# A last chunk of 64 columns: two label steps side by side in the partitions, row tanh by transposes, two stores on another queue

## The chip, the cores and the metric

The kernel runs on one core of a Trainium2 chip. The time is the device time of one execution in microseconds; the kernel before has a median of 795.49 us over three runs (794.16 to 795.92). A profile of one more execution goes with it.

## The reference

A speech "joint" network, forward and backward, in bf16. x is (2, 16000, 256), g is (2, 8, 256), the incoming gradient is (2, 4000, 8, 256).

```
h  = gelu(conv3(x,  w1))[:, ::2, :]        # 16000 -> 8000 steps
f  = gelu(conv3(h,  w2))[:, ::2, :]        # 8000 -> 4000 steps
fe = f @ w_f ;  ge = g @ w_g               # (2,4000,256), (2,8,256)
j  = tanh(fe[:, :, None, :] + ge[:, None, :, :])   # (2,4000,8,256)
out = j @ w_o                              # (2,4000,8,256)
```

Returned are out and the gradients of x, w1, w2, g, w_f, w_g and w_o for the given gradient of out. The joint j has 8 label steps u for each of the 2 x 4000 time steps; its products with w_o, in both directions, and the gradient of w_o are most of the work.

## The kernel before, in words

**Tiling.** The 8000 time steps (both batches in a row) are cut into chunks: one of 256, fifteen of 512, and a last one of 64 (`sizes`). A chunk of 512 is held as A = 4 blocks of Pw = 128 steps, the last as A = 1 block of Pw = 64. Most tensors of a chunk stand with the features in the partitions and the steps in the free dimension (JT, FE, NGFE, GF, GHe, GHo and so on). Products that sum over time steps need the steps in the partitions; those copies are called rows and end in R (JR, FER, NFR, GFR, GHoR, GHeR, HRo, HRe, FR).

**Stages.** For each k the program records three stages, `stage_j(k)` (the joint), `stage_a(k+1)` (both convolutions, FE) and `stage_de(k-1)` (the backward pass through the convolutions and the weight gradients), so that in steady state three chunks are in work at once. At the end, `gg_out` makes the gradients of g, w_g and w_o.

**The joint of a chunk**, for each pair `up` of label steps u = 2 up and 2 up + 1: ScalarE makes JT = tanh(FE + GE) with the features in the partitions (L644). The same values with the steps in the partitions, JR, are made anew: VectorE adds FER and GEB (L668), ScalarE takes the tanh (L673). Chunks 0 and 1 (`TRANS`) instead transpose JT on TensorE into PSUM (L663) and copy the result out. TensorE then does, per pair: GWO += JR' x GO (the gradient of w_o, kept in one PSUM bank for the whole kernel), ps = WOT x GOT (the gradient with respect to j), out = JT' x WO. GO is the incoming gradient with the steps in the partitions, GOT its transpose by DMA. VectorE multiplies by 1 - j^2 (JSQ, L716) into ZS and NGZ and adds up to NGFE (L730, L733); ScalarE or VectorE copies out of PSUM to OUT_SB (L345, L350), and a DMA stores it.

In the last chunk one GO tile of 64 partitions holds all eight u (64 x 2048), one DMA transpose makes GOT from it, and each u is handled on its own with 64 partitions: out is 64 x 512 per pair (two u in the free dimension), GWO takes four matmuls per pair with 64 rows of JR each.

**stage_de** goes NGFE -> (WFT) GF -> (W2T) GHe, GHo -> (W1T) the gradient of x (GX_SB, stored by `put`), with the row copies NFR, GFR, GHeR, GHoR made on the way for the weight gradients: NFR with FR, GFR with HRe and HRo, GHoR and GHeR with X (loaded by `load_x`). For all but the last chunk these rows are made by DMA transposes on SyncE's queue; they share two buffers (`rows`), so GHeR waits until NFR has been read and GHoR until GFR has. For the last chunk TensorE transposes them (L489). The sums of the weight gradients live in ACCF, ACC2 and ACC1 in SBUF (L772); with the last chunk VectorE writes them to `stage` tiles (L764), which are stored, all on SyncE's queue but the very last, which ScalarE issues.

**What sets the order.** Operations are recorded with a cost estimate and a due time; the planner `Flow.issue` plays the engines forward, picks at each step the operation that can start first (ties by due time), and so writes a fixed order for each engine. Each engine and each DMA queue then works strictly in that order. PSUM has seven banks handed out in any order; other tiles have one to three buffers per class. A few operations may run on either ScalarE or VectorE (`evac`, JSQ); the planner picks. So an edit in one stage can move instructions of its neighbours. Nearly all DMAs, loads, stores and transposes, go through SyncE's one queue (L360, L362). In the last 40 us that queue holds, in order: the last GO load, OUT stores, NFR, GOT, GFR, the X load of the second last chunk, GHeR, OUT stores, GHoR, HRo, GX stores, the X load of the last chunk (two DMAs, one of a single row), the two small stores of g's gradient (`JR` 8 x 256, of `gg_out`), and the stores of g_sq, stage and GX_SB.

Of the kernel before, what the change touches and what calls it, by code (L numbers as in the profile page):

```python
# [220 lines left out]
def kernel(  # L221
# [198 lines left out]
    def load_go(k, up, at, after=()):  # L420
        c = chunks[k]
        A, Pw = c.A, c.Pw
        GO = buf("go", [P, NB, 2, V], BF16, "GO")
        if c.last:

            dma("SP", lambda: GO[:Pw].rearrange("p a u v -> p (a u v)"),
                lambda: bass.AP(tensor=go_.tensor, offset=go_.offset + c.c0 * U * V, ap=[[U * V, Pw], [1, U * V]]),
                r=[], w=[GO], bytes_=Pw * U * V * 2, new=[GO], at=at, after=after)
            st[k]["GO"] = {up: GO for up in range(UP)}
            return  # L430
        dma("SP", lambda: GO[:Pw, 0:A].rearrange("p a u v -> p a (u v)"),
            lambda: bass.AP(tensor=go_.tensor, offset=go_.offset + (c.c0 * U + 2 * up) * V,
                            ap=[[A * U * V, Pw], [U * V, A], [1, 2 * V]]),
            r=[], w=[GO], bytes_=Pw * A * 1024, new=[GO], at=at, after=after, sub="go")
        st[k].setdefault("GO", {})[up] = GO

    def load_got(k, up, at):
# [4 lines left out]
        if c.last:  # L442
            dma("SP", lambda: GOT[:, :, :, :, :Pw].rearrange("p a u k c -> p (a u k) c"),
                lambda: GO[:Pw].rearrange("p a u v -> p (a u v)"), r=[GO], w=[GOT],
                bytes_=Pw * U * V * 2, new=[GOT], transpose=True, at=at)
# [92 lines left out]
    def stage_a(k, t0, dt):  # L538
# [45 lines left out]
        for mt in range(KT):  # L584
# [6 lines left out]
            evac(lambda mt=mt: FE[:, 0:A, mt, :Pw], lambda ps=ps: fl(ps[:, :W], A), W, r=[ps], w=[(FE, mt)])  # L591
        if k not in TRANS:
            S["FER"] = rows(k, "fer", "FER", FE, 0, A, [(FE, 0), (FE, 1)], pe=Pw, lag=0.0 if c.first else 500.0)
# [4 lines left out]

    n_gwo = sum(len(c.blk) for c in chunks) * U * KT
    gwo_cnt = [0]  # L600
# [27 lines left out]
    def stage_j(k, t0, dt, GEB):  # L628
# [3 lines left out]
        FE = S["FE"]  # L632

        def pair(up):
            F.now = tu = t0 + dt * up / UP
            q = dt / UP
            JT = buf("jt", [P, 2, KT, CW], BF16, "JT")
            GOT, GO = S["GOT"].pop(up), S["GO"].pop(up)
            u0 = up if c.last else 0
            for j in range(2):  # L640
                for mt in range(KT):
                    def jt(e, j=j, mt=mt):
                        for b, lo, hi, _ in c.segs:
                            nc.scalar.activation(  # L644
                                out=fl(JT[:, j, mt, :W], A)[:, :, lo:hi], in_=FE[:, 0:A, mt, lo:hi], func=ACT.Tanh,
                                bias=GE[:, b, mt, 2 * up + j:2 * up + j + 1], scale=1.0)
# [4 lines left out]
            for h, tbs in enumerate(halves):  # L651
                JR = buf("jr", [P, 2, 2, D], BF16, "JR")
                th = tu + q * (h / 2 - 0.5)
                n, lo, m = len(tbs), tbs[0][0], Pw
                if k in TRANS:
                    tr = psum(BF16)
# [27 lines left out]
                op("PE", c_pe([V] * (4 * n)), gwo, r=[JR, GO], w=[], at=tu + q * (h / 2 + 0.3), sub="gwo")  # L684
            OUT = buf("out", [P, NB, 2, V], BF16, "OUT_SB")
            for step in range(4):
# [5 lines left out]
                def gj(e, j=j, d2=d2, ps=ps):  # L692
                    for kt in range(KT):
                        mm(fl(ps[:, :W], A), WOT[:, kt, d2 * P:(d2 + 1) * P], GOT[:, u0:u0 + A, j, kt, :Pw], kt == 0, kt == KT - 1)
                if u and d2 == 0:
                    NGZ = buf("ngz", [P, KT, CW], FP32, "NGZ")
                op("PE", c_pe([W] * KT), gj, r=[GOT, WOT], w=[ps], new=[ps, NGZ] if u and d2 == 0 else [ps])
                if d2 == 0:
                    JSQ = buf("jsq", [P, KT, CW], BF16, "JSQ")

                    def jsq(e, j=j, JSQ=JSQ):
                        if e == "ACT":
                            nc.scalar.activation(out=JSQ[:, :, :W], in_=JT[:, j, :, :W], func=ACT.Square)  # L703
                        else:
                            nc.vector.tensor_tensor(out=JSQ[:, :, :W], in0=JT[:, j, :, :W], in1=JT[:, j, :, :W], op=ALU.mult)
                    op(("ACT", "DVE"), (c_act(KT * W), c_dve(KT * W, 0.5)), jsq, r=[(JT, (j, 0)), (JT, (j, 1))], w=[JSQ],
# [69 lines left out]
    def stage_de(k, t0, dt):  # L776
# [136 lines left out]
        for bl, m in c.sblk:  # L913
# [21 lines left out]
            if bl % 2 == 1 or bl == A - 1:  # L935
# [201 lines left out]
```

## Time and profile before

| | |
|---|---|
| median of the runs | 795.49 us (794.16 to 795.92) |
| the profiled execution | 793.3 us |
| its span, first to last instruction | 791.0 us |
| TensorE, VectorE, ScalarE busy | 773.1, 716.1, 727.0 us |
| SyncE's hardware DMA queue | 177.03 of 178.82 MB |
| granted TensorE clock | 0.998 |
| last chunk's first joint work on TensorE beside the chunk before | from 753.88 us |
| last idle stretch of TensorE ahead of its end | 1.09 us at 777.4 us, waiting for NGFE |
| VectorE's last instruction ends | 786.66 us |
| SyncE's last DMA issue | 787.80 us |

A line of the timeline reads: start in us, duration in us, engine, source line, operation, output<-inputs, shape, count. For TensorE the shape in front (128*64) is that of the stationary weights, partitions times columns, and the next that of the moving operand. Matmuls overlap, so their price is read from one start to the next and not from the durations. L336 is the helper that issues all matmuls but the transposes, L360 and L362 the helper that issues DMAs (SPq is SyncE's queue, ACTq ScalarE's). Brackets show idle time of the engine just before and what ended it.

### The profile page before, as it was taken

Reading aid. Unit: us, or ns where it says so; the run is one execution under the profiler, and the core shown is the slowest. Engines: PE = TensorE matmul, PEld = TensorE weight load, DVE = VectorE, ACT = ScalarE, POOL = GpSimd, SP = SyncE. Lnnn points to the kernel's source line nnn. Section 1 sums busy time; section 2 is a strip of 40 time slices with the busy share of each in tenths; the row PEclk is TensorE's granted clock in tenths of the full one; section 3 lists DMA queues with packets and bytes.
Section 4 is the critical chain, followed back from the end, with each engine's and each line's share of the span. In section 5 each row is a group of like instructions: output and inputs, shape, how many; then the busy total and the mean of one; then the engine's idle time right before and its main releaser. Section 6 shows DMA issues by size and latency. Waiting matters only on the chain.

```text
span 791.0 us, 15682 instructions
## 1 busy us (share of the span) xinstructions
PE 773.1 (98%) x5687; PEld 537.9 (68%) x5722; DVE 716.1 (91%) x1514; ACT 727.0 (92%) x1176; POOL 83.8 (11%) x227
## 2 busy tenths in 40 slices
PE   8989999999999999999999999999999999999996
PEld 6657577576675767767677675776767767577764
DVE  5899999897998989999999898989989899899874
ACT  6999999999999998999999998999999999898752
POOL 2110010201002011110101102010020110102010
PEclk9999999999999999999999999999999999999999
DMA  9999999999999899999999999998999999999874
GB/s 208 205 190 202 214 263 229 244 228 281 202 231 256 231 238 195 229 267 219 233 218 254 228 217 233 214 264 209 230 235 214 239 237 228 237 264 255 201 177 123
DMA packets 381809, 178.82 MB, mean 226 GB/s; under 512 B 307586, under 2 KB 375460, under 8 KB 379812
## 3 DMA queue, kind: packets, MB, share of 16 engines
q1 hardware_dynamic: 380516, 177.03, 99.8%
q8 instruction: 45, 0.74, 0.4%
q10 hardware_dynamic: 1056, 0.52, 0.2%
q14 instruction: 32, 0.26, 0.1%
q0 software_dynamic: 160, 0.27, 0.1%
HBM read 51.42 MB, written 50.34 MB: 129 GB/s over the span
## 4 chain that ended last, share of the span: by engine, by line
PE 72%; ACT 11%; DVE 9%; DMA 3%; issue 3%; SPq 1%; POOL 0%; DVEq 0%; ACTq 0%
PE ps L336 60%; PE GWO L336 10%; ACT JT L644 2%; DVE g_s L516 2%; ACT JSQ L703 2%; DMA GOT<-GO 2%; ACT g_sq L510 2%; PE psb L489 2%; DVE NGZ L716 1%; ACT OUT_SB L345 1%; ACT JR L673 1%; DVE g_sq L529 1%; SPq L360 1%; ACT HTo L513 1%; DMA XC<-in_x_dram 1%
## 5 line engine op out<-in xcount | busy, mean ns | idle before, releaser
L644 ACT ACTIVATE JT<-FE,GE 128x512 bf16<-128x512 bf16 (+4 forms) x288 | 180.7, 680 | 0.0
L716 DVE SCALAR_TENSOR_TENSOR NGZ<-JSQ,ps 128x512 f32<-128x512 bf16 (+3 forms) x252 | 149.7, 607 | 2.5 <-PE ps L336 2.0
L336 PE MATMUL ps<-WO,JT 128*128 128x256 bf16 (+1 forms) x1008 | 148.2, 273 | 1.3 <-DVE NGZ L716 1.3
L336 PE MATMUL ps<-GOT,WOT 128*128 128x512 bf16 (+2 forms) x544 | 146.5, 362 | 1.8 <-DMA GOT<-GO 1.6
L345 ACT CAST OUT_SB<-ps 128x512 bf16<-128x512 f32 (+1 forms) x210 | 123.0, 600 | 17.4 <-PE ps L336 17.3
L703 ACT ACTIVATE JSQ<-JT 128x1024 bf16<-128x1024 bf16 (+2 forms) x128 | 128.6, 1005 | 9.2 <-DVE NGZ L716 8.2
L336 PEld LDWEIGHTS <-JT 128*128 128x128 bf16 (+1 forms) x1008 | 98.2, 98 | 54.9 <-issue 2.0
L336 PE MATMUL GWO<-GO,JR 128*128 128x256 bf16 (+1 forms) x1008 | 130.8, 273 | 0.1
L673 ACT ACTIVATE JR<-JR 128x1024 bf16<-128x1024 bf16 (+1 forms) x116 | 121.6, 1054 | 4.1 <-DVE JR L668 3.8
L733 DVE TENSOR_TENSOR ZS<-ZS,NGZ 128x1024 f32<-128x1024 f32 (+2 forms) x102 | 115.1, 1128 | 0.3
L336 PEld LDWEIGHTS <-JR 128*128 128x128 bf16 (+1 forms) x1008 | 98.2, 98 | 17.8 <-issue 1.3
L516 DVE SCALAR_TENSOR_TENSOR g_s<-g_sq,ps 128x512 bf16<-128x512 bf16 (+2 forms) x102 | 65.2, 639 | 41.0 <-ACT HTo L513 32.2
L336 PEld LDWEIGHTS <-W 128*128 128x128 bf16 x612 | 58.1, 98 | 59.5 <-issue 2.2
L336 PE MATMUL ps<-XC,W 128*128 128x512 bf16 (+2 forms) x408 | 84.3, 362 | 0.9 <-DMA XC<-in_x_dram 0.9
L668 DVE TENSOR_TENSOR JR<-FER,GEB 128x1024 bf16<-128x1024 bf16 (+1 forms) x116 | 79.2, 684 | 2.2 <-PE GWO L336 1.0
L336 PEld LDWEIGHTS <-X 128*128 128x128 bf16 (+1 forms) x756 | 73.8, 98 | 9.4
L772 DVE TENSOR_TENSOR ACC<-ACC,ps 128x512 f32<-128x512 f32 x90 | 59.4, 678 | 16.9 <-PE ps L336 16.7
L336 PEld LDWEIGHTS <-WOT 128*128 128x128 bf16 x544 | 51.6, 98 | 23.9 <-DMA GOT<-GO 1.8
L347 ACT ACTIVATE GX_SB<-ps 128x512 bf16<-128x512 f32 (+1 forms) x109 | 64.1, 615 | 1.6 <-PE ps L336 1.1
L510 ACT ACTIVATE g_sq<-ps 128x512 bf16<-128x512 f32 (+2 forms) x102 | 59.1, 580 | 3.4 <-PE ps L336 2.7
L525 ACT ACTIVATE g_s<-g_s 128x1024 bf16<-128x1024 bf16 (+2 forms) x51 | 52.1, 1025 | 6.3 <-DVE g_s L516 6.1
L336 PE MATMUL ps<-GHoR,X 128*128 128x256 bf16 (+1 forms) x378 | 57.7, 273 | 0.0
(139 smaller groups left out, 1113.6 us busy)
## 6 DMA issues: line engine op xcount, KB each, us to landing
GO<-in_grad_out_dram SPq DMA_DIRECT2D x60, 512.0 KB, 5.3
out_dram<-OUT_SB SPq DMA_DIRECT2D x60, 512.0 KB, 5.3
X<-in_x_dram SPq DMA_DIRECT2D x15, 1088.0 KB, 8.3
out_dram<-GX_SB SPq DMA_DIRECT2D x30, 512.0 KB, 5.5
GO<-in_grad_out_dram SPq DMA_DIRECT2D x5, 256.0 KB, 5.4
GOT<-GO SPq DMA_TRANSPOSE x65, 5.0
out_dram<-OUT_SB SPq DMA_DIRECT2D x4, 256.0 KB, 3.5
XC<-in_x_dram SPq DMA_TRANSPOSE x62, 5.5
```

What stands on the lines that cost most here:

```text
L336: nc.tensor.matmul(ps_ap, lhsT=lhsT, rhs=rhs, start=start, stop=stop)
L345: nc.scalar.copy(out=dst(), in_=src())
L347: nc.scalar.activation(out=dst(), in_=src(), func=ACT.Copy, scale=scale)
L510: op("ACT", c_act(W, True), lambda e, mt=mt, ps=ps: nc.scalar.activation(out=sq[:, 0:A, mt, :Pw], in_=fl(ps[:, :W], A), func=ACT.Square, s ...
L516: op("DVE", c_dve(W), lambda e, mt=mt, ps=ps: nc.vector.scalar_tensor_tensor(out=s[:, 0:A, mt, :Pw], in0=sq[:, 0:A, mt, :Pw], scalar=1.0, ...
L644: nc.scalar.activation(out=fl(JT[:, j, mt, :W], A)[:, :, lo:hi], in_=FE[:, 0:A, mt, lo:hi], func=ACT.Tanh, bias=GE[:, b, mt, 2 * up + j:2 ...
L668: op("DVE", c_dve(n * 2 * D, 0.5), lambda e, lo=lo, n=n, m=m, JR=JR: nc.vector.tensor_tensor(out=JR[:m, 0:n], in0=S["FER"][:m, lo:lo + n]. ...
L673: op("ACT", c_act(n * 2 * D), lambda e, n=n, m=m, JR=JR: nc.scalar.activation(out=JR[:m, 0:n], in_=JR[:m, 0:n], func=ACT.Tanh), r=[JR], w= ...
L703: nc.scalar.activation(out=JSQ[:, :, :W], in_=JT[:, j, :, :W], func=ACT.Square)
L716: nc.vector.scalar_tensor_tensor(out=fl(zap(), A)[:, :, lo:hi], in0=fl(JSQ[:, d2, :W], A)[:, :, lo:hi], scalar=1.0, in1=fl(ps[:, :W], A)[: ...
L733: nc.vector.tensor_tensor(out=a, in0=a, in1=b, op=ALU.add)
L772: op("DVE", c_dve(512), lambda e: nc.vector.tensor_tensor(out=acc_ap().rearrange("p k d -> p (k d)"), in0=acc_ap().rearrange("p k d -> p ( ...
```

## The change

In the last chunk the two u of a pair now stand side by side in the partitions, 2 x 64 = 128:

- GO: partitions 0 to 63 hold the even u, 64 to 127 the odd ones, four u each. Two DMAs load it, in pieces of 512 bytes. GOT is made from 128 partitions with half the columns.
- JT of a pair holds both u side by side in its columns (`jtw`), 128 columns. FER is not made for this chunk, and JR is no longer FER + GEB with a tanh, but JT transposed on TensorE (two transposes per pair) and copied out by ScalarE or VectorE.
- GWO takes two matmuls per pair with 128 rows instead of four with 64; out takes two with 128 columns of weights instead of four with 64, into a 128 x 256 PSUM tile; its copy is 128 x 256. One OUT tile holds all pairs and is stored by two DMAs at the end of the chunk, in pieces of 512 bytes, instead of four stores.
- The store of the last chunk's gradient of x (two DMAs) is issued on ScalarE's queue instead of SyncE's.

The products with GOT (64 columns), JSQ and the chain to NGFE have the same sizes as before. All other chunks are unchanged. The planner's order changes with it in the last 60 us. On SyncE's queue, the two small JR stores now stand ahead of the last chunk's two X loads. On TensorE, the last products with GOT stand ahead of the block of GHoR,X and GHeR,X matmuls of the second last chunk instead of behind it, and the ngb matmuls of `gg_out` stand between that block and NGFE,WFT. On VectorE, the three adds to ACC1 of that block stand behind the ngb copies, and two stage evictions stand ahead of GHo. One group of GX matmuls moves ahead of the products with GOT, and one behind them.

```diff
@@ load_go
-            dma("SP", lambda: GO[:Pw].rearrange("p a u v -> p (a u v)"),
-                lambda: bass.AP(tensor=go_.tensor, offset=go_.offset + c.c0 * U * V, ap=[[U * V, Pw], [1, U * V]]),
-                r=[], w=[GO], bytes_=Pw * U * V * 2, new=[GO], at=at, after=after)
+            for j in range(2):
+                dma("SP", lambda j=j: GO[j * Pw:(j + 1) * Pw].rearrange("p a u v -> p (a u v)")[:, 0:UP * V].rearrange(
+                        "p (a v) -> p a v", v=V),
+                    lambda j=j: bass.AP(tensor=go_.tensor, offset=go_.offset + (c.c0 * U + j) * V,
+                                        ap=[[U * V, Pw], [2 * V, UP], [1, V]]),
+                    r=[], w=[(GO, j)], bytes_=Pw * UP * V * 2, new=[GO] if j == 0 else [], at=at, after=after)
@@ load_got
-            dma("SP", lambda: GOT[:, :, :, :, :Pw].rearrange("p a u k c -> p (a u k) c"),
-                lambda: GO[:Pw].rearrange("p a u v -> p (a u v)"), r=[GO], w=[GOT],
+            dma("SP", lambda: GOT[:].rearrange("p a u k c -> p (a u k) c")[:, 0:UP * KT, 0:2 * Pw],
+                lambda: GO[:2 * Pw].rearrange("p a u v -> p (a u v)")[:, 0:UP * V], r=[GO], w=[GOT],
@@ stage_a
-        if k not in TRANS:
+        if k not in TRANS and not c.last:
             S["FER"] = rows(k, "fer", "FER", FE, 0, A, [(FE, 0), (FE, 1)], pe=Pw, lag=0.0 if c.first else 500.0)
@@ stage_j
+        def jtw(JT, j):
+            return JT[:, 0, :, j * W:(j + 1) * W] if c.last else JT[:, j, :, :W]
+
...
-                if k in TRANS:
+                if c.last:
+                    tr = psum(BF16)
+
+                    def trs(e, tr=tr):
+                        for kt in range(KT):
+                            nc.tensor.transpose(out=tr[:2 * Pw, kt * P:(kt + 1) * P], in_=JT[:, 0, kt, :2 * Pw], identity=ident[:])
+                    op("PE", c_pe([P] * KT), trs, r=[JT, ident], w=[tr], new=[tr], at=th, sub="jr")
+                    evac(lambda JR=JR: JR[:2 * Pw, 0, 0], lambda tr=tr: tr[:2 * Pw, 0:D], D, r=[tr], w=[JR], new=[JR], f=0.58)
+                elif k in TRANS:
...
-                        for j in range(2):
+                        for j in range(1 if c.last else 2):
                             for d2 in range(KT):
                                 n = gwo_cnt[0]
-                                mm(GWO[:, d2, :], JR[:m, tb % 2, j, d2 * P:(d2 + 1) * P], GO[:m, up if c.last else tb, j, :],
+                                rhs = (GO[:2 * m].rearrange("p a u v -> p (a u v)")[:, up * V:(up + 1) * V] if c.last
+                                       else GO[:m, tb, j, :])
+                                mm(GWO[:, d2, :], JR[:2 * m if c.last else m, tb % 2, j, d2 * P:(d2 + 1) * P], rhs,
                                    n == 0, n == n_gwo - 1)
...
+                    if c.last:
+                        def out_last(e, m=m, ps=ps):
+                            for kt in range(KT):
+                                mm(ps[:2 * m, 0:V], JT[:, 0, kt, :2 * m], WO[:, kt, :], kt == 0, kt == KT - 1)
+                        op("PE", c_pe([V] * 2), out_last, r=[JT, WO], w=[ps], new=[ps] + ([OUT] if up == 0 else []), sub="out")
+                        evac(lambda m=m: OUT[:2 * m, up, 0], lambda m=m, ps=ps: ps[:2 * m, 0:V], V, r=[ps], w=[(OUT, up)])
+                        continue
...
+            if c.last:
+                for j in range(2 if up == UP - 1 else 0):
+                    dma("SP", lambda j=j: bass.AP(tensor=o_.tensor, offset=o_.offset + (c.c0 * U + j) * V,
+                                                  ap=[[U * V, Pw], [2 * V, UP], [1, V]]),
+                        lambda j=j: OUT[j * Pw:(j + 1) * Pw, 0:UP, 0], r=[OUT], w=[], bytes_=Pw * UP * V * 2)
+                return
@@ stage_de, put
-                    dma("SP", lambda: row_ap(gx_, row + 4 * A * p0 + lo, 4 * A, p1 - p0, hi - lo),
+                    dma("ACT" if c.last else "SP", lambda: row_ap(gx_, row + 4 * A * p0 + lo, 4 * A, p1 - p0, hi - lo),
```

More of the change, by code (lines that the diff above doesn't have):

```diff
@@ L597, in stage_a @@
         S["FR"] = rows(k, "fr", "FR", FT, 0, A, None, pe=Pw)
-    n_gwo = sum(len(c.blk) for c in chunks) * U * KT
+    n_gwo = sum(len(c.blk) * (UP if c.last else U) for c in chunks) * KT
     gwo_cnt = [0]
@@ L638, in pair @@
             GOT, GO = S["GOT"].pop(up), S["GO"].pop(up)
-            u0 = up if c.last else 0
             for j in range(2):
@@ L644, in jt @@
                             nc.scalar.activation(
-                                out=fl(JT[:, j, mt, :W], A)[:, :, lo:hi], in_=FE[:, 0:A, mt, lo:hi], func=ACT.Tanh,
+                                out=fl(jtw(JT, j)[:, mt], A)[:, :, lo:hi], in_=FE[:, 0:A, mt, lo:hi], func=ACT.Tanh,
                                 bias=GE[:, b, mt, 2 * up + j:2 * up + j + 1], scale=1.0)
@@ L677, in gwo @@
                     for tb, m in tbs:
-                        for j in range(2):
+                        for j in range(1 if c.last else 2):
                             for d2 in range(KT):
                                 n = gwo_cnt[0]
-                                mm(GWO[:, d2, :], JR[:m, tb % 2, j, d2 * P:(d2 + 1) * P], GO[:m, up if c.last else tb, j, :],
+                                rhs = (GO[:2 * m].rearrange("p a u v -> p (a u v)")[:, up * V:(up + 1) * V] if c.last
+                                       else GO[:m, tb, j, :])
+                                mm(GWO[:, d2, :], JR[:2 * m if c.last else m, tb % 2, j, d2 * P:(d2 + 1) * P], rhs,
                                    n == 0, n == n_gwo - 1)
                                 gwo_cnt[0] = n + 1
-                op("PE", c_pe([V] * (4 * n)), gwo, r=[JR, GO], w=[], at=tu + q * (h / 2 + 0.3), sub="gwo")
-            OUT = buf("out", [P, NB, 2, V], BF16, "OUT_SB")
+                op("PE", c_pe([V] * (2 if c.last else 4 * n)), gwo, r=[JR, GO], w=[], at=tu + q * (h / 2 + 0.3), sub="gwo")
+            OUT = S["OUT"] if c.last and up else buf("out", [P, NB, 2, V], BF16, "OUT_SB")
+            S["OUT"] = OUT
             for step in range(4):
@@ L693, in gj @@
                     for kt in range(KT):
-                        mm(fl(ps[:, :W], A), WOT[:, kt, d2 * P:(d2 + 1) * P], GOT[:, u0:u0 + A, j, kt, :Pw], kt == 0, kt == KT - 1)
+                        rhs = (GOT[:].rearrange("p a u k c -> p (a u k) c")[:, up * KT + kt:up * KT + kt + 1, j * Pw:(j + 1) * Pw]
+                               if c.last else GOT[:, 0:A, j, kt, :Pw])
+                        mm(fl(ps[:, :W], A), WOT[:, kt, d2 * P:(d2 + 1) * P], rhs, kt == 0, kt == KT - 1)
                 if u and d2 == 0:
@@ L702, in jsq @@
                         if e == "ACT":
-                            nc.scalar.activation(out=JSQ[:, :, :W], in_=JT[:, j, :, :W], func=ACT.Square)
+                            nc.scalar.activation(out=JSQ[:, :, :W], in_=jtw(JT, j), func=ACT.Square)
                         else:
-                            nc.vector.tensor_tensor(out=JSQ[:, :, :W], in0=JT[:, j, :, :W], in1=JT[:, j, :, :W], op=ALU.mult)
+                            nc.vector.tensor_tensor(out=JSQ[:, :, :W], in0=jtw(JT, j), in1=jtw(JT, j), op=ALU.mult)
                     op(("ACT", "DVE"), (c_act(KT * W), c_dve(KT * W, 0.5)), jsq, r=[(JT, (j, 0)), (JT, (j, 1))], w=[JSQ],
```

## The prediction

> **What bounds the kernel now.** I read the page's engine shares first, then the table of stretches for the last ninety microseconds, because the diff only touches the last chunk and the changed kernel's instruction order is the same on every engine until about 734 us (TensorE: equal up to its row 10629 of 11446). The page:
>
> ```profile
> span 791.0 us, 15682 instructions
> PE 773.1 (98%) x5687; PEld 537.9 (68%) x5722; DVE 716.1 (91%) x1514; ACT 727.0 (92%) x1176; POOL 83.8 (11%) x227
> ```
>
> TensorE is busy for 98% of the span. Its matmuls overlap, so that figure alone proves little; the stretches by engine (columns: length, PE, PEld, DVE, ACT, POOL busy us with counts, clock, DMA share, GB/s) say where it really has no gap:
>
> ```profile
> 740.00:755.00 15.00, 14.95 (x122) 11.77 (x121) 11.87 (x25) 9.18 (x21) 0.00 (x0) 1.00 0.62 192
> 755.00:765.00 10.00, 9.86 (x74) 5.70 (x74) 8.00 (x25) 3.85 (x12) 2.09 (x7) 1.00 0.98 240
> 765.00:777.40 12.40, 12.34 (x111) 9.54 (x109) 5.69 (x26) 5.29 (x11) 0.00 (x0) 1.00 0.69 175
> 777.40:785.00 7.60, 6.49 (x60) 4.08 (x61) 5.90 (x24) 4.01 (x10) 1.75 (x6) 1.00 0.15 42
> ```
>
> Up to 777.4 TensorE's stream is the bound; VectorE and ScalarE have 3 us and more to spare per stretch. So a matmul removed there is time removed, unless something else is late. Behind 777.4 stands a dependent chain (the last chunk's backward pass), and behind that the stores. The next view is TensorE's timeline where the last chunk's 64-row work sits:
>
> ```profile
> 753.88 1.06 PE L336 MATMUL ps<-WO,JT 128*64 128x256 bf16 x8
> 754.88 0.61 PE L336 MATMUL ps<-NGFE,WFT 128*128 128x512 bf16 x2
> 755.42 0.61 PE L336 MATMUL GWO<-GO,JR 64*128 64x256 bf16 x4
> 755.96 0.60 PE L336 MATMUL ps<-NGFE,WFT 128*128 128x512 bf16 x2
> 756.50 1.04 PE L336 MATMUL GWO<-GO,JR 64*128 64x256 bf16 x8
> 757.47 1.04 PE L336 MATMUL ps<-GF,W2T 128*128 128x512 bf16 x4
> 758.44 0.61 PE L336 MATMUL GWO<-GO,JR 64*128 64x256 bf16 x4
> ```
>
> Read the starts. Four GWO matmuls with 64-row weights take 755.42 to 755.96, 0.54 us, and eight take 0.97; eight with full weights take 0.87 elsewhere (745.07 to 745.94). Two NGFE matmuls of 512 columns take 0.54 where a pair takes 0.43 at 768.44. So a 256-column matmul costs 0.109 us whatever its weight's size, and each change between a 64-wide and a full weight costs 0.10 to 0.11 us more.
>
> The end, SyncE's and ScalarE's stores and the last VectorE work:
>
> ```profile
> 773.03 0.85 SPq L362 DMA_DIRECT2D X<-in_x_dram  x2
> 779.93 0.66 SPq L362 DMA_DIRECT2D out_dram<-JR  x2
> 784.78 1.88 DVE L764 SCALAR_TENSOR_TENSOR stage<-ACC,ps 128x512 bf16<-128x512 f32 x3 [0.45 <-PE ps L336]
> 786.04 0.48 SPq L362 DMA_DIRECT2D out_dram<-GX_SB  x1
> 786.61 1.14 SPq L362 DMA_DIRECT2D out_dram<-stage  x2
> 786.70 0.42 ACTq L362 DMA_DIRECT2D out_dram<-stage  x1
> 787.80 0.40 SPq L362 DMA_DIRECT2D out_dram<-GX_SB  x1
> ```
>
> VectorE is done at 786.66, but SyncE issues back to back, about 0.55 us each from 783.0 on, and starts its last store at 787.80. The waits of SyncE's queue show 1.5 us on that store's landing (to 789.7); the span ends 1.3 later.
>
> **The change, part by part, in the clock of this trace.**
>
> Out matmuls: 16 become 8 of 128 rows, saving 8 x 0.109 = 0.87. GWO matmuls: 16 become 8, another 0.87. The two FER transposes go: full-weight work ends at 734.10 and resumes at 734.42, 0.32. Six stretches of 64-wide weights (the lines above, and four-matmul WO,JT groups at 761.68 and 770.60) become full: 12 changes x 0.105 = 1.26. Added: eight JT transposes. This row shows their price, since chunks 0 and 1 already use them:
>
> ```profile
> 19.91 0.61 PE L663 MATMUL psb<-ident,JT 128*128 128x128 bf16 x8
> 20.36 0.60 PE L336 MATMUL ps<-WO,JT 128*128 128x256 bf16 x4
> ```
>
> Eight take 19.91 to 20.36, so +0.45. The Trainium skill, page "TensorE: Matmul & The Clock Gate", section "Part 4: PE-mode transpose", speaks against this part: it gives some 275 ns for one 128x128 transpose within a kernel. By that figure, as an estimate, eight would cost 2.2 us and the whole gain would shrink by 1.75; the trace shows 0.055 us from start to start, so the trace decides.
>
> Two waits give some back. (1) After the last full GOT,WOT (ends 752.48) VectorE needs one NGZ and two NGFE, ending 754.59, 2.1 later, plus some 0.05 to TensorE. The changed order fills TensorE with WO,JT 0.43, GWO 0.87, four transposes 0.22 and four out matmuls 0.44, 1.97 in all: a wait of 0.18. Queued behind is everything. (2) The fourth row transpose needs the last JT. ScalarE from 753.60 does a JSQ (0.21), two JT (0.46), one JR copy and two half OUT copies (0.8, half of the 64x512 forms' cost), six JT (1.32): 756.4. TensorE arrives at 756.26: 0.2. The evictions that replace the VectorE adds and ScalarE tanhs (0.36 and 0.53 each busy; the new 256-element copies about 0.27) are no dearer and sit off the path. GF's second half on VectorE is ready 1.87 after the first NGFE matmul; that is where TensorE comes out anyway.
>
> So the block of GHoR,X and GHeR,X matmuls that starts at 771.82 starts 0.87+0.87+0.32+1.26-0.45-0.18-0.2 = 2.5 earlier, at 769.3, and ends at 774.55 instead of 777.12 (a GOT pair inside it moved out).
>
> Three transfers must keep up with that. NFR is issued when NGFE is done and needed 5.25 later; the NFR of the chunk before landed in 5.3: nothing, bounded above by 0.85 (it was in place when first used, 6.1 after its issue). GHoR waits for the last GFR matmul, in the old run 766.51, needed 5.3 later; now the filler between is 4.14, as one out group is gone and one GX group stands ahead. Landings of such transposes in the trace: GHeR 3.3, GFR 3.9, GOT 4.1 to 5.2. HRo, issued 768.47 right behind it, landed 2.5 later. I take nothing, bound 1.2. GO in two DMAs of 512-byte pieces: SyncE idles between 747.74 and 753.73, and GOT needs it at 756.3: nothing; at worst it lands like a whole GO, 7.4, by 755.2.
>
> Tail, from the block's end to VectorE's end: 9.54 before. The NGFE wait of 1.09 goes, as the last GOT groups stand ahead of the block; its place is taken by the small ngb matmuls. Counting starts in the new order (each narrow group 0.11 for the change plus its columns): ngb pairs 0.66, WFT 0.22, NGFE transposes 0.22, JR,GR 0.32, GF transposes 0.22, then W2T at 1.74 after the block, 2.98 before. VectorE's ACC add, JR copy and two GF (0.6+0.3+0.28) fit under that. Then VectorE has two stage evictions ahead of GHo, the first behind the second JR,GR, so TensorE waits 0.4 for GHo before its last transposes. I count 8.27 to VectorE's end: 1.27 saved.
>
> Moved on SyncE: the last chunk's two X loads now stand behind the two JR stores, which wait for the ngb results. They would be issued at 776.5 and land 3.0 later (this load's row), 779.5; first use 780.3. Hidden with 0.8 to spare. Stores: SyncE loses two GX issues, so the last issue is ScalarE's stage at VectorE's end + 0.04 instead of 1.14 after it: 1.1 saved, but a 128 KB store lands in 2.2 where the small GX took 1.9: 0.8 net. ScalarE issues its GX stores at about 781; nothing but the stage store is behind them.
>
> Sum: 2.55 + 1.27 + 0.8 = 4.6. The profiled execution took 793.3 us (span 791.0 and 2.3 around it), so 788.7 (span 786.4). It lies 2.2 below the median of the runs; against the median the forecast is 795.49 - 4.6 = 790.9.
>
> **The rivals.**
> - Late rows: GHoR (and NFR) land as late as the bounds allow and TensorE stands before the block. GOT's 5.2 speaks for it, HRo's 2.5 against. Gain 4.6-1.2 = 3.4, 792.1; with NFR 792.9.
> - The change of weight shape is no price of its own, but an effect of how ends are modelled: gain 4.6-1.26-0.2 = 3.1, 792.4. Against it: the extra 0.1 appears at each such change and nowhere else.
> - Nothing measurable: the X load lands like the 16-row X loads of the page, 8.3 us, at 784.8. That is 4.5 after its first use, and 795.4 results.
> - Slower, by the same load: from a landing of 8.4 us on, the GX and weight matmuls of the last chunk wait longer than was won. The trace bounds the X load of the chunk before only by 11.9 (issued 759.88, used 771.82); with that, 788.4, 8.1 late, 799.0. Against it: 160 KB instead of 1088, idle DMA engines then (0.15 share), and 3.0 measured.
>
> **Numbers.** Forecast 0.6, late rows 0.18, no shape price 0.08, nothing 0.08, slower 0.06. About 0.2% (1.6 us) is what a measurement of this kernel can tell from no change. The first three are faster: 0.86; same 0.08, slower 0.06. Low end: without the three waits (0.8) the gain is 5.4, 790.1, and the runs spread by 0.8: 789.3. High end: late rows with both bounds, 792.9, and 0.7 for spread: 793.6.
>
> **What would show it.** Right: no 128*64 or 64*128 matmuls of JT and JR, GHoR,X restarting near 769.3 without idle ahead, the wait on NGFE L730 gone, VectorE's end near 782.8, SyncE's last issue ahead of ScalarE's. Wrong: idle on TensorE ahead of GHoR,X or NFR,FR put down to a DMA; a wait on the X load in the last matmuls; transposes further apart than 0.06; or the second half of the kernel slowed by an engine that I left out.

## The result, and the profile after

The changed kernel takes 790.44 us (median of 7 runs, 788.14 to 793.89), the kernel before 794.16 in the runs beside it (7 runs, 792.32 to 795.92). The ratio is 0.9955, with a 95% interval of 0.9933 to 0.9977; the medians differ by 3.7 us. The forecast was 4.6 us and 790.9: the time is inside the range, the gain a fifth smaller than the sum.

The profiled execution took 788.95 us, with this page:

```profile
span 786.3 us, 15688 instructions
PE 772.4 (98%) x5712; PEld 537.4 (68%) x5712; DVE 715.1 (91%) x1510; ACT 725.0 (92%) x1175; POOL 83.8 (11%) x227
```

The span fell by 4.7, but not all of that is the change. The first 733 us are the same program, so two executions should agree there, and they don't: the VectorE add JR<-FER,GEB that stands last before the orders part starts at 733.61 before and at 732.71 after. I call its start the anchor; before, then after:

```profile
733.61 0.68 DVE L668 TENSOR_TENSOR JR<-FER,GEB 128x1024 bf16<-128x1024 bf16 x1
```

```profile
732.71 0.68 DVE L681 TENSOR_TENSOR JR<-FER,GEB 128x1024 bf16<-128x1024 bf16 x1
```

Over all profiles shown here it lies between 732.51 and 736.10, so spans of single executions are not compared below, only times counted from the anchor:

| from the anchor (us) | before | after | after, second profile |
|---|---|---|---|
| anchor itself | 733.61 | 732.71 | 732.51 |
| start of the block of GHoR,X matmuls | 38.21 | 36.41 | 36.20 |
| end of that block | 43.51 | 41.64 | 41.44 |
| end of VectorE's last instruction | 53.05 | 50.04 | 49.84 |
| end of the span | 57.39 | 53.59 | 53.59 |

So the change is worth 3.80 us behind the anchor in both profiles, which is what the runs say (3.7). Split as the prediction split it: 1.87 and 2.07 up to the block's end (predicted 2.55), 1.14 in both from there to VectorE's end (1.27), 0.79 and 0.59 behind it (0.8).

The stretches of the changed kernel, cut where its block (774.60) and VectorE's work (783.00) have just ended (length, busy time of PE, PEld, DVE, ACT, POOL with counts, clock, DMA share, GB/s):

```profile
740.00:755.00 15.00, 15.00 (x125) 11.70 (x123) 11.15 (x22) 8.26 (x23) 0.00 (x0) 1.00 0.64 201
755.00:765.00 10.00, 9.72 (x85) 6.87 (x85) 8.15 (x30) 3.11 (x10) 2.09 (x7) 1.00 1.07 244
765.00:774.60 9.60, 9.34 (x85) 7.18 (x83) 5.53 (x30) 3.29 (x7) 0.00 (x0) 1.00 0.69 165
774.60:783.00 8.40, 6.97 (x64) 4.35 (x62) 6.27 (x15) 4.62 (x11) 1.77 (x6) 1.00 0.42 117
```

TensorE is still the engine without slack up to 774.6, but the second and third stretch now miss 0.28 and 0.26 us where they missed 0.14 and 0.06 before. TensorE's timeline says what these are:

```profile
752.55 0.28 PE L665 MATMUL psb<-ident,JT 128*128 128x128 bf16 x2
752.66 0.38 PE L336 MATMUL ps<-WO,JT 128*128 128x256 bf16 x2
...
753.21 0.59 PE L336 MATMUL ps<-NGFE,WFT 128*128 128x512 bf16 x2
...
754.62 0.38 PE L336 MATMUL ps<-WO,JT 128*128 128x256 bf16 x2
755.19 0.47 PE L665 MATMUL psb<-ident,JT 128*128 128x128 bf16 x2 [0.19 <-ACT JT L649]
755.50 1.03 PE L336 MATMUL ps<-GF,W2T 128*128 128x512 bf16 x4
...
768.52 0.34 PE L336 MATMUL ps<-GOT,WOT 128*128 128x64 bf16 x6
769.12 0.60 PE L336 MATMUL ps<-GHoR,X 128*128 128x256 bf16 x4 [0.26 <-DMA GHoR<-GHo]
```

There are no 64-wide weights left in this part. Two transposes take 0.11 from start to start (752.55 to 752.66), the 0.055 each of the prediction. At 755.19 TensorE waits for ScalarE's last JT, and at 769.12 for GHoR. For the second wait the starts say more than the 0.26 in the bracket: six GOT matmuls with 64 columns take 0.17 (from 770.76 to 770.94 in a kernel further down, where the block has nothing to wait for), so the block could have started at 768.69 and started 0.43 later. The chain that ended last shows the same transfer:

```profile
764.52 4.46 DMA GHoR<-GHo
768.98 0.14 issue
769.12 5.71 PE ps L336 x50
```

The tail, in the timeline of TensorE, and then VectorE's part of it:

```profile
775.20 0.29 PE L336 MATMUL ps<-NGFE,WFT 128*128 128x64 bf16 x4
...
778.28 0.30 PE L492 MATMUL psb<-ident,GHe 128*65 128x128 bf16 x2
778.72 0.38 PE L492 MATMUL psb<-ident,GHo 128*65 128x128 bf16 x2
...
780.23 0.27 PE L336 MATMUL ps<-GHoR,X 65*128 65x256 bf16 x1
```

```profile
778.45 0.35 DVE L881 SCALAR_TENSOR_TENSOR GHo<-G1o,ps 128x65 bf16<-128x65 bf16 x2
...
780.87 1.88 DVE L796 SCALAR_TENSOR_TENSOR stage<-ACC,ps 128x512 bf16<-128x512 f32 x3 [0.89 <-PE ps L336]
```

NGFE,WFT has no idle time ahead of it any more. In the kernel before it had 1.09:

```profile
777.12 0.28 PE L336 MATMUL ps<-GOT,WOT 128*128 128x64 bf16 x4
778.48 0.38 PE L336 MATMUL ps<-NGFE,WFT 128*128 128x64 bf16 x4 [1.09 <-DVE NGFE L730]
```

And the queues of SyncE and ScalarE after the change:

```profile
775.26 0.70 SPq L362 DMA_DIRECT2D out_dram<-JR  x2
776.02 0.83 SPq L362 DMA_DIRECT2D X<-in_x_dram  x2
...
779.33 4.16 SPq L362 DMA_DIRECT2D out_dram<-stage  x5
781.05 1.25 ACTq L362 DMA_DIRECT2D out_dram<-GX_SB  x2
782.79 0.40 ACTq L362 DMA_DIRECT2D out_dram<-stage  x1
```

VectorE ends at 782.75. SyncE's last issue ends at 783.49, 0.74 behind it; before it was 788.20, 1.54 behind.

### The profile page after: what moved, and what is told of

Read it like the earlier page. It is cut to its first block, busy times and chain, and to the rows that moved or that the text cites. A ratio compares the mean times of both kernels' runs of the same rounds, so it can differ in the third digit from the quotient of the medians.

```text
span 786.3 us, 15688 instructions
## 1 busy us (share of the span) xinstructions
PE 772.4 (98%) x5712; PEld 537.4 (68%) x5712; DVE 715.1 (91%) x1510; ACT 725.0 (92%) x1175; POOL 83.8 (11%) x227
## 4 chain that ended last, share of the span: by engine, by line
PE 68%; ACT 14%; DVE 11%; DMA 3%; issue 3%; SPq 0%; POOL 0%; DVEq 0%; ACTq 0%; POOLq 0%
PE ps L336 57%; PE GWO L336 10%; ACT JT L649 3%; DVE g_s L519 3%; ACT JSQ L721 2%; ACT OUT_SB L345 2%; DVE NGZ L734 2%; ACT g_sq L513 2%; DMA GOT<-GO 2%; PE psb L492 1%; ACT JR L686 1%; DVE g_sq L532 1%; ACT HTo L516 1%; ACT GX_SB L347 1%; DMA XC<-in_x_dram 1%
## 5 line engine op out<-in xcount | busy, mean ns | idle before, releaser
L336 PE MATMUL ps<-WO,JT 128*128 128x256 bf16 x1000 | 147.3, 273 | 1.3 <-DVE NGZ L734 1.3
L336 PEld LDWEIGHTS <-JT 128*128 128x128 bf16 x1000 | 97.4, 98 | 54.4 <-issue 1.6
L336 PE MATMUL GWO<-GO,JR 128*128 128x256 bf16 x1000 | 130.1, 273 | 0.1
L686 ACT ACTIVATE JR<-JR 128x1024 bf16<-128x1024 bf16 x112 | 119.1, 1069 | 3.2 <-DVE JR L681 3.0
L336 PEld LDWEIGHTS <-JR 128*128 128x128 bf16 x1000 | 97.7, 98 | 17.4 <-DVE JR L350 0.3
L681 DVE TENSOR_TENSOR JR<-FER,GEB 128x1024 bf16<-128x1024 bf16 x112 | 77.4, 693 | 2.2 <-PE GWO L336 1.0
L336 PE MATMUL ps<-W1T,GHo 128*128 128x512 bf16 (+1 forms) x252 | 61.3, 326 | 0.0
```

The costliest lines, as they stand in the source:

```text
L336: nc.tensor.matmul(ps_ap, lhsT=lhsT, rhs=rhs, start=start, stop=stop)
L681: op("DVE", c_dve(n * 2 * D, 0.5), lambda e, lo=lo, n=n, m=m, JR=JR: nc.vector.tensor_tensor(out=JR[:m, 0:n], in0=S["FER"][:m, lo:lo + n]. ...
L686: op("ACT", c_act(n * 2 * D), lambda e, n=n, m=m, JR=JR: nc.scalar.activation(out=JR[:m, 0:n], in_=JR[:m, 0:n], func=ACT.Tanh), r=[JR], w= ...
```

## The experiments

Every experiment is read from its anchor. Times in the table are us from it, except the first column. Each row is one profile. The two profiles of the changed kernel differ by 0.21 at the block's start and by 0.20 between VectorE's end and the span's end, so a difference of that size between two rows says nothing. In the rows "out twice, full" and "before, last rows by transposes" the granted clock fell behind the block (see below); their last two columns are not compared.

| kernel | anchor | block start | VectorE's end | span's end |
|---|---|---|---|---|
| before | 733.61 | 38.21 | 53.05 | 57.39 |
| after | 732.71 | 36.41 | 50.04 | 53.59 |
| out 64-wide again | 733.91 | 37.26 | 50.90 | 54.79 |
| out twice, full | 735.45 | 36.48 | 51.80 | 54.65 |
| GX stores back on SyncE | 732.93 | 36.66 | 50.30 | 54.37 |
| before, GX stores on ScalarE | 733.90 | 38.20 | 53.04 | 57.20 |
| before, last rows by transposes | 734.08 | 38.55 | 56.33 | 59.12 |
| GHoR in a buffer of its own | 733.26 | 36.00 | 49.64 | 53.44 |
| the same, order left to the planner | 736.10 | 35.81 | 50.67 | 55.10 |
| JT in small buffers | 733.09 | 36.63 | 50.27 | 54.01 |
| GHo ahead of a stage eviction | 732.78 | 36.27 | 49.50 | 52.92 |
| all three repairs | 735.49 | 35.45 | 48.68 | 52.21 |

### Does a change of the weights' shape have a price?

The prediction put 1.26 us of its sum down to twelve changes between 64-wide and full weights; a rival said that there is no such price. Two kernels with the same number of matmuls and columns differ on TensorE only in that (off it, the copies and stores of out differ in form). One makes out with 64-wide weights again (sixteen matmuls), the other makes every full-width out matmul twice (sixteen as well, the second with the same values):

```
 64-wide:
-  mm(ps[:2 * m, 0:V], JT[:, 0, kt, :2 * m], WO[:, kt, :], ...)
+  for jj in range(2):
+      mm(ps[:m, jj * V:(jj + 1) * V], JT[:, 0, kt, jj * m:(jj + 1) * m], WO[:, kt, :], ...)
 twice:
+  for _ in range(2):
       for kt in range(KT):
           mm(ps[:2 * m, 0:V], JT[:, 0, kt, :2 * m], WO[:, kt, :], kt == 0, kt == KT - 1)
```

> The changed kernel with the last chunk's out matmuls undone alone: 16 matmuls of 64 weight columns instead of 8 of 128, each group with a change of weight shape on both sides. Count theory with a price for the shape: 8 x 0.109 + 8 x 0.105 = 1.7 longer than 53.6, 55.3, or 55.0 if the wait ahead of the fourth row transpose (0.35) swallows a part. Rival (the shape has no price): 0.9 or 0.5 longer, 54.1 to 54.5. In the timeline the starts ahead of and behind these groups are 0.1 further apart by the first, and 0.109 per matmul by the second.

> The changed kernel with every out matmul of the last chunk done twice with its full weights (the second writes the same values again): the same number of matmuls as with 64-wide weights and no change of shape. Both theories: 8 x 0.109 = 0.87 longer or, where the wait of 0.35 swallows a part, 0.5: 54.1 to 54.5. The difference to the run with 64-wide weights is the shape's price: 0.84 by mine, 0 by the rival.

The same place in TensorE's timeline, first with 64-wide weights:

```profile
753.75 0.27 PE L665 MATMUL psb<-ident,JT 128*128 128x128 bf16 x2
753.96 0.62 PE L336 MATMUL ps<-WO,JT 128*64 128x256 bf16 x4
754.51 0.29 PE L665 MATMUL psb<-ident,JT 128*128 128x128 bf16 x2
```

then with full ones:

```profile
755.29 0.28 PE L665 MATMUL psb<-ident,JT 128*128 128x128 bf16 x2
755.40 0.60 PE L336 MATMUL ps<-WO,JT 128*128 128x256 bf16 x4
755.84 0.27 PE L665 MATMUL psb<-ident,JT 128*128 128x128 bf16 x2
755.95 0.60 PE L336 MATMUL ps<-WO,JT 128*128 128x256 bf16 x4
756.39 0.59 PE L336 MATMUL ps<-NGFE,WFT 128*128 128x512 bf16 x2
```

Four matmuls take 0.44 in the second (755.40 to 755.84) and 0.55 in the first (753.96 to 754.51); the transposes ahead of them 0.11 and 0.21, since the change from full to 64-wide lies between. So such a group pays 0.21 for its two changes. The 64-wide kernel reaches its block 0.78 later (37.26 against 36.48), although its wait for JT is 0.11 shorter: from its last transposes to GF,W2T it takes 0.17 (757.36 to 757.53) and the doubled kernel 0.28 (758.24 to 758.52), where two transposes need 0.11. So eight changes more cost 0.89, or 0.11 each, which is the 0.105 of the sum. The price stands in the starts and delays the block; it is not a matter of modelled ends. This rival falls.

The 64-wide kernel's span ended at 54.79, earlier than the 55.0 to 55.3 expected: of the 1.76 of work that it has more than the changed kernel (eight matmuls and eight changes) only 0.85 shows at the block (37.26 against 36.41). Two waits took in the rest, as the other kernel shows.

The doubled kernel also teaches what an added matmul costs. Its eight matmuls should put the block 0.87 later than after's; it came 0.07 later, because two waits took them in. GHoR's wait of 0.43 is gone, and the wait for JT has shrunk by 0.38 (from 0.55 to 0.17): from the first NGFE,WFT to GF,W2T this kernel takes 2.13 (756.39 to 758.52) with two matmuls more in between, the changed kernel 2.29. The three add up to 0.88. TensorE "98% busy" and even "no gap in the stretch" do not mean that each matmul counts in full.

Its tail, from the block's start to VectorE's end, took 15.32 instead of 13.63. The stretches show why (columns as above; the last but two is the clock):

```profile
780.00:782.00 2.00, 1.86 (x19) 1.11 (x18) 1.94 (x5) 1.44 (x3) 0.64 (x3) 0.94 0.53 146
782.00:784.00 2.00, 2.00 (x7) 1.01 (x6) 0.80 (x2) 0.96 (x2) 0.00 (x0) 0.50 0.60 170
784.00:786.00 2.00, 2.00 (x15) 1.51 (x13) 0.63 (x2) 0.59 (x1) 0.00 (x0) 0.71 0.61 168
```

The granted clock was 0.50 between about 781.8 and 785.2, and matmuls of 256 columns started 0.21 us apart instead of 0.11. The tail has the same instructions as that of the changed kernel, whose two profiles kept 1.00 there, so the longer tail is no price of the doubled matmuls by themselves. Whether the added work ahead of it has a part in the fall of the clock, one profile cannot show. The tail of this kernel is therefore not compared.

### What is moving the GX stores worth?

Moved back to SyncE in the changed kernel, and moved alone in the kernel before:

```
 changed kernel:
-  dma("ACT" if c.last else "SP", lambda: row_ap(gx_, ...), ...)
+  dma("SP", lambda: row_ap(gx_, ...), ...)
 kernel before:
-  dma("SP", lambda: row_ap(gx_, ...), ...)
+  dma("ACT" if c.last else "SP", lambda: row_ap(gx_, ...), ...)
```

> The changed kernel with one part undone: the last chunk's two GX stores are back on SyncE's queue; the other engines keep their order. I measure from the start of the VectorE add to JR that stands last before the two kernels' orders part (733.61 before, 732.71 after) to the end of the span: 57.4 before, 53.6 after. My theory (the end hangs on SyncE's issue time): two issues of 0.53 more on SyncE, last issue about 1.1 after VectorE's end again, 0.8 longer, 54.4; nothing ahead of VectorE's end changes. Rival (the bytes of the last stores must drain anyway): 53.6, no change.

> The kernel before with this one part of the change alone: the last chunk's two GX stores on ScalarE's queue. By the issue theory 0.8 shorter than 57.4, 56.6, and 0.8 of some 3.7 is what this part gives by itself; by the drain theory 57.4. If it gives much more than 0.8, the rest of the change is worth less than I think.

Back on SyncE, the span ends 0.78 later from the anchor, as expected, but 0.25 of that is already there at the block's start (36.66 against 36.41), ahead of everything that the edit touches; that 54.4 came out is in part luck. Behind VectorE's end it takes 4.07, against 3.55 and 3.75 in the two profiles of the changed kernel: 0.3 to 0.5. Alone in the kernel before it gives 4.16 instead of 4.34 there: 0.2, no more than two profiles of one kernel differ by, where I had expected 0.8. The queues of that kernel show why:

```profile
785.59 2.41 SPq L362 DMA_DIRECT2D out_dram<-stage  x4
...
786.98 0.40 ACTq L362 DMA_DIRECT2D out_dram<-stage  x1
```

SyncE still issues stage stores until 788.00, 1.06 behind VectorE's end (786.94). Both GX issues are gone from the queue, but it was backlogged by the other stores, and the queue's end moved only from 1.54 to 1.06 behind VectorE's end. The rest of the gain behind VectorE's end must come with the rest of the change. What I can see of it is that the first g_sq store is issued 4.95 ahead of VectorE's end in the changed kernel (777.80) and 3.66 ahead before (783.00), so that the queue is freer when the last stage stores come. No run tests that by itself, but the kernel whose order is left to the planner (below) agrees with it. It has all the edited lines, the GX stores on ScalarE among them, and nearly the old order in the tail. Its first g_sq store is again issued 3.66 ahead of VectorE's end (783.11, end at 786.77), and its span ends 4.43 behind that end, no sooner than the kernel before. By these profiles the gain behind VectorE's end, too, hangs on the tail's order more than on the queue of the GX stores.

### Is the row part worth anything alone?

The kernel before with the last chunk's rows made by transposes of its 64-wide JT (sixteen transposes, no FER), without laying two u side by side:

```
-    TRANS = (0, 1)
+    TRANS = (0, 1, 16)
```

> The kernel before with the last chunk's row tanh by TensorE transposes alone, in its 64-wide form: 16 transposes with 64-wide weights in four groups, no FER, no adds, no second tanh. By my prices: FER's 0.32 goes, 16 x 0.055 = 0.88 comes, and some four to eight changes of shape (0.4 to 0.8) where the groups stand among full weights: 0.9 to 1.4 longer than 57.4, 58.3 to 58.8, so that this part alone would lose and only pays with the 128 partitions. Rival (the relief of VectorE and ScalarE is what the change lives on): shorter than 57.4.

The block came 0.34 later, not 0.9 to 1.4. The 0.33 of FER's transposes had been won by the first joint group of the last chunk (753.88 before, 754.02 here, so 20.27 and 19.94 from the anchor), and from there to the block it lost 0.67, less than sixteen transposes at 0.055 (0.88). The 0.2 between lies in the first group of products with GOT: fourteen of them take 0.75 in the kernel before (762.24 to 762.99), here twelve take 0.45 (762.31 to 762.76) and two that stand later some 0.06. Why that group is shorter here is not shown. So the transposes do not pay by themselves, and the rival (the relief of VectorE and ScalarE) falls as far as the block. In the changed kernel, where two u share each transpose, eight cost 0.45 and FER's 0.32 goes, still no gain; what the row part brings is the 128 rows that halve GWO and make its weights full. Behind the block this execution too had the clock at 0.50:

```profile
784.00:786.00 2.00, 2.00 (x10) 1.07 (x11) 1.88 (x3) 1.60 (x4) 0.00 (x0) 0.50 0.43 124
```

so its tail says nothing.

### GHoR: is its wait a loss, and what makes it late?

GHoR shares its two buffers with GFR, so its transpose is issued when the last GFR matmul is done (764.52). The second-last chunk's GHoR gets the buffers of FER, which the last chunk no longer uses. Left to itself the planner then moves the block ahead of the last GOT group, as in the kernel before; so there are two kernels, one with the changed kernel's order kept:

```
 both:
-  GHoR = rows(k, "rows", "GHoR", GHo, ...)
+  GHoR = rows(k, "fer" if k == NG - 2 else "rows", "GHoR", GHo, ...)
 order kept, on the matmuls of ACC1's weight gradient:
+  behind=[F.last_gj] if k == NG - 2 and ACC is ACC1 else []
```

> The changed kernel; the GHoR of the second last chunk gets a buffer of its own (one that FER no longer needs), so its transpose need not wait until GFR has been read. All engines keep their order but SyncE, where GHoR stands ahead of the OUT stores. In the profile of the changed kernel TensorE waits 0.26 for GHoR (0.43 by the starts) ahead of the GHoR,X block. Theory (that wait is a loss on the path): it goes, and from the same anchor 53.6 becomes 53.2. Rival (something else is due at the same moment, such as the X load or HRo): another wait in its place, 53.5 to 53.6.

> The same buffer, but the planner is left to choose: it puts the GHoR,X block ahead of the last products with GOT again, as in the kernel before. My theory says that the order 'GOT products first' is worth what the tail gained beyond fewer matmuls (the NGFE wait of 1.09 and two shape changes): so some 0.8 to 1.2 longer than with the kept order, 54.0 to 54.4, with idle on TensorE ahead of NGFE,WFT. Rival (the order is worth nothing, the chain behind is the same length): within 0.2 of the kept order.

With the order kept, TensorE has no wait there:

```profile
769.26 0.60 PE L336 MATMUL ps<-GHoR,X 128*128 128x256 bf16 x4
```

The block starts at 36.00 from the anchor, 0.41 earlier, which is where the wait-free count of the changed kernel put it (35.98), and VectorE ends 0.40 earlier: the wait is a loss in full up to there. Only 0.15 of it reaches the end of the span: the last stores took 3.80 behind VectorE's end instead of 3.55, within what two profiles of the changed kernel differ by.

With the order left free the wait for NGFE of the kernel before is back, in TensorE's timeline:

```profile
778.58 0.38 PE L336 MATMUL ps<-NGFE,WFT 128*128 128x64 bf16 x4 [1.08 <-DVE NGFE L748]
```

VectorE's end is 1.03 and the span's end 1.66 later than with the order kept, the latter more than the 0.8 to 1.2 expected. From the block's end to VectorE's end this kernel takes 9.55, as the kernel before does (9.54), against 8.40. So all of the tail's gain (1.14) is a matter of order: the last GOT groups, and VectorE's sums behind them, stand ahead of the block instead of behind it. The ngb matmuls and the stage evictions moved together with them, and no run parts these. The edited lines do not ask for that order. It hangs on a buffer: with another buffer for one tile the planner gives it up.

### JT earlier: GHoR's wait grows

The wait at 755.19 came from ScalarE's tanh of the last pairs. In the changed kernel the last chunk's JT uses the full chunk's buffers and ScalarE's timeline has the last six JT here:

```profile
753.83 1.55 ACT L649 ACTIVATE JT<-FE,GE 128x64 bf16<-128x64 bf16 x6
```

With four small buffers they can run earlier:

```
-  JT = buf("jt", [P, 2, KT, CW], BF16, "JT")
+  JT = buf("jtl", [P, 1, KT, P], BF16, "JT") if c.last else buf("jt", [P, 2, KT, CW], BF16, "JT")
```

> The changed kernel; the last chunk's JT get four small buffers of their own, so that ScalarE can make them before the buffers of the chunk before come free. In the changed kernel TensorE stood 0.35 ahead of the fourth row transpose until the last JT was done. Theory: that goes; from the anchor to the start of the GHoR,X block 0.35 less, unless the wait for GHoR, which hangs on the GFR matmuls and moves with them, grows: so 0.2 to 0.35 less at the block, 53.6 becomes 53.3. Rival (VectorE's GF is due at the same moment): no change, TensorE then waits for GF ahead of GF,W2T.

```profile
768.37 0.34 PE L337 MATMUL ps<-GOT,WOT 128*128 128x64 bf16 x6
769.72 0.60 PE L337 MATMUL ps<-GHoR,X 128*128 128x256 bf16 x4 [1.02 <-DMA GHoR<-GHo]
```

In this timeline TensorE gets through its work ahead of the block 0.53 earlier than in the changed kernel (35.45 from the anchor without the wait, against 35.98), and then stands 1.18 before GHoR, issued at 764.37 and landing 5.2 us later. No wait stands ahead of GF,W2T any more, so the rival (VectorE's GF) falls. The block starts 0.22 later than in the changed kernel, the span's end is 0.4 later. GHoR was issued 0.53 earlier, too, right behind the GFR matmuls (31.28 from the anchor against 31.81); had it landed in 4.46 again, the wait would have stayed at 0.43 and the block would have come 0.53 earlier. So in this execution it is the longer landing that took JT's repair back. Whether the earlier issue made it longer, or chance did, is not shown by one profile. With GHoR's wait not mended, the repair of JT's can't be relied on.

### GHo ahead of a stage eviction

In the tail VectorE makes a second stage eviction before GHo, and TensorE waits for GHo (its transposes start 0.44 behind those of GHe above, where two take 0.11). One wait by order puts GHo first:

```
+  F.gho = op("DVE", ... GHo ...)
   stage eviction of ACC2:
+  behind=[F.gho] if ACC is ACC2 else []
```

> The changed kernel with one stage eviction on VectorE moved from ahead of the last chunk's GHo to behind it. In the profile of the changed kernel GHo's matmuls are done about 778.0, but VectorE starts GHo at 778.45 and TensorE waits for it. Theory: GHo starts 0.4 earlier, the wait of 0.3 on TensorE goes, 53.6 becomes 53.3. Rival (VectorE's work ahead of the last three stage evictions is the bound, and only moves): 53.6.

VectorE's end in this kernel:

```profile
780.40 1.88 DVE L796 SCALAR_TENSOR_TENSOR stage<-ACC,ps 128x512 bf16<-128x512 f32 x3 [0.37 <-PE ps L336]
```

From the block's end to VectorE's end it takes 7.99 instead of 8.40, so 0.41 is won, and the rival (VectorE's work is the bound) falls. This is the 0.4 that the prediction put down for the wait for GHo, found where it said. The span ends 0.67 earlier from the anchor, but the other 0.26 stands outside the edit: 0.14 is there at the block's start, 0.13 behind VectorE's end.

### All three repairs, and a second profile of the changed kernel

GHoR's own buffer with the order kept, small JT buffers, and GHo first, together:

> The changed kernel with the three repairs together: GHoR in a buffer of its own, JT in small buffers, GHo ahead of the second stage eviction. If the three waits (0.4, 0.35, 0.3 to 0.5) lie one behind the other on the path, 1.1 to 1.2 less than 53.6, 52.4, and some 0.6% below the kernel before in the rounds (ratio 0.994). Rival (one takes the place of the other, or the stores' issue takes over as the bound): 53.0 or more, and a ratio no better than the changed kernel's 0.9955.

> The changed kernel as it is, once more, to see how far the measure from the anchor repeats. If it is as exact as I use it, 53.6 within 0.3 to the end of the span, 50.0 within 0.2 to VectorE's end; the wait for GHoR and the landing of the last stores are the parts that may move. If TensorE's clock falls in the tail, as it did in two of the runs so far, VectorE's end comes 1.5 to 3 later.

TensorE's timeline at the two places, and VectorE's end:

```profile
770.76 0.34 PE L337 MATMUL ps<-GOT,WOT 128*128 128x64 bf16 x6
770.94 0.60 PE L337 MATMUL ps<-GHoR,X 128*128 128x256 bf16 x4
...
780.10 0.30 PE L493 MATMUL psb<-ident,GHe 128*65 128x128 bf16 x2
780.24 0.28 PE L493 MATMUL psb<-ident,GHo 128*65 128x128 bf16 x2
```

```profile
782.29 1.88 DVE L797 SCALAR_TENSOR_TENSOR stage<-ACC,ps 128x512 bf16<-128x512 f32 x3 [0.38 <-PE ps L337]
```

None of the three waits is left: six GOT matmuls and the block are 0.18 apart, the GHo transposes follow the GHe ones by 0.14. The block starts 35.45 from the anchor, the span ends at 52.21, 1.38 before the changed kernel's. JT's repair, which came out at -0.4 alone, now gives its 0.5 (36.00 with GHoR mended alone, 35.45 here). The median is 788.68 us (6 runs, 787.1 to 789.9) against 793.89 for the kernel before (11 runs, 791.94 to 795.62): ratio 0.9928, 0.9909 to 0.9947. Its median lies 5.2 us below that of the kernel before, against 3.7 for the changed kernel; its interval overlaps the changed kernel's (0.9933 to 0.9977) a little, so the runs alone don't prove the further gain. The second profile of the changed kernel took 788.7 us and gave the fourth column of the first table: GHoR's wait 0.19 instead of 0.43, and the same 53.59 (expected 53.6 within 0.3).

## Why the prediction was right, step by step

**What bounds it.** Right: TensorE's stream up to the block, a dependent chain behind it, then the stores. One reading is off: from 755 to 765 VectorE has 2.0 us to spare (8.00 busy of 10.00), not 3 and more; nothing hung on it.

**Halved matmuls, FER, shape changes, transposes** (0.87, 0.87, 0.32, 1.26, -0.45). Right in mechanism and size, as far as measured: transposes at 0.055, shape changes at 0.11 where 0.105 was taken, and the last full GOT,WOT 0.34 earlier from the anchor, which is FER's 0.32. The Trainium skill (page "TensorE: Matmul & The Clock Gate", section "Part 4: PE-mode transpose") gives some 275 ns for a transpose within a kernel; by that figure, as an estimate, the gain would have been 1.75 smaller. The row of the trace was right (0.11 for two). The kernel with all three repairs bears out the whole count, since its stream up to the block has no wait left: its block starts 2.76 earlier than before (35.45 against 38.21), where these five terms make 2.87.

**A term that the sum left out.** In the new order 32 products with GOT stand ahead of the block, and 26 did before. The last six take 0.17 (770.76 to 770.94 with all repairs). The sum counts only a pair of them that left the block, as a gain.

**The NGFE wait of 0.18.** It did not come. NGFE,WFT starts at 753.21, 1.97 after the end of the last full GOT,WOT (751.24), the very filler that was counted, with no idle time. VectorE was not faster than forecast. Its timeline has the two halves of NGFE, and the second ends 2.1 behind that GOT,WOT, as predicted:

```profile
752.06 1.29 DVE L748 TENSOR_TENSOR NGFE<-ZS,NGZ 128x512 bf16<-128x512 f32 x2
```

That is 753.35, 0.14 after TensorE has begun. The first matmul reads only the first half, which ended at 752.75; the prediction was wrong in letting TensorE wait for both.

**The fourth row transpose, 0.2.** Undersized. From the first NGFE,WFT (753.21) to GF,W2T (755.50) TensorE took 2.29 where 1.94 follows from the prediction. ScalarE's six JT took 1.55, where I had counted 1.32, and the last was done later than TensorE came. That is 0.35 more; 0.18 of it is the NGFE wait that did not come, since TensorE arrived earlier by as much.

**GHoR in time, taken as nothing, bound 1.2.** This is the largest step that failed, and one of the prediction's own signs of being wrong came with it: idle time ahead of GHoR,X, put down to a DMA. The filler was counted right, but I chose the short landings (GHeR 3.3, GFR 3.9) over those of GOT (4.1 to 5.2); GHoR landed after 4.46 and TensorE stood 0.43 (0.19 in the second profile, 1.18 with JT mended, all inside the bound). So the rival of late rows was partly true. NFR was in time, and GO in two pieces showed no wait of GOT in this part. Together 0.43 + 0.35 - 0.18 = 0.60, and with the 0.17 of the six GOT products 0.77. The profile fell short by 0.69 at the block's start (1.80 instead of 2.49) and the second one by 0.48 (0.53 by the same sum, with its wait of 0.19).

**The tail, 1.27.** It gave 1.14. The mechanism is shown: with the order of the tail turned back, the NGFE wait of 1.08 returns; with GHo put first, 0.41 is won.

**The X load behind JR's stores.** Right: the second issue starts at 776.3, lands 2.7 later at 779.0, first use 780.23 (predicted 776.5, 779.5, 780.3). The two rivals that lived on this load, nothing and slower, fall.

**Stores, 0.8.** The sum came out (0.79 and 0.59), the step did not: SyncE's last issue ends 0.30 behind ScalarE's and not ahead of it, and the GX stores are worth 0.3 to 0.5 of it in this kernel and alone no more than 0.2. By the kernel whose order was left to the planner, the rest goes with the tail's order.

**The total.** 4.6 forecast, 3.80 behind the anchor, 3.7 by the runs. That the profiled span (786.3) hit the forecast of 786.4, and VectorE's end (782.75) that of 782.8, is luck: that execution was 0.9 ahead of the other at the anchor, which made up for what the block lacked. That the median of 790.44 lies so near to 790.9 is in part luck, too: the forecast started from 795.49, and the kernel before had 794.16 in the runs beside it.

## What to carry to other kernels

Give a transfer's landing the range that its kind shows in the trace, and if the work that covered it shrinks, take the middle and not the short end: here the cover of GHoR shrank from 5.3 to 4.1 us, transfers of its kind had landed in 3.3 to 5.2, and the 4.46 that it took became a wait. Ask of each wait that is taken away what stands next (behind JT's wait stood GHoR's), and mend them together. When the order changes, count what moved ahead of the point that you forecast, and not only what was added or taken away. And compare single profiles only from a point where both ran the same code; the last microseconds of a kernel hang on orders and buffers that the edit does not name.

## What the hardware showed unexpectedly

- In 2 of 13 profiles the granted clock of TensorE was 0.50 for 3.4 and 6.8 us inside the tail (the doubled out and the row transposes alone); from the block's end to VectorE's end they took 1.7 and 2.9 us longer than the changed kernel and the kernel before. The other profiles of these two tails kept it until TensorE's last matmul. Both have more TensorE work ahead of it than their neighbours, but so has the kernel with out 64-wide, which kept its clock. What sets it off stays open.
- Up to the anchor the same code differs by 3.6 us between executions (732.51 to 736.10), as much as the whole change.
- The same DMA transpose of GHoR landed 4.46 us after its issue in one execution and 5.2 in another, of two kernels with the same transfers in the same order ahead of it on its queue.
- Changing between 64-wide and full weights costs TensorE 0.11 us per change (0.89 for eight), as much as a 256-column matmul (0.109).
